# Attention: low parts of three transpose banks per pair on GpSimd instead of VectorE, and GpSimd's other work in another order

## The chip, the cores and the metric

One core of one Trainium2 chip runs the whole program. The metric is the device time of one execution in microseconds (us); the text gives the median of three runs. One further execution was recorded by the hardware profiler, and all rows below come from it.

## The reference

`q`, `k`, `v` are (2, 8, 768, 64): 16 heads. Each head gets a bucket number per token from the signs of six projections, and attention is allowed only inside a bucket. Two feed-forward blocks follow, each on 1536 tokens, 512 wide, with 2048 hidden columns.

```python
q_bits = (einsum('bhsd,dk->bhsk', q, proj) > 0); k_bits = the same of k
mask   = q_bucket[:, :, :, None] == k_bucket[:, :, None, :]
scores = where(mask, D**-0.5 * q @ k.T, -1e9)
attn   = exp(scores - max(scores)); attn = attn / (sum(attn) + 1e-9)
x      = attn @ v                        # to (1536, 512)
h      = maximum(x @ moe_w_in, 0);  x = h * h @ moe_w_out
h      = x @ moe2_w_in;             out = (h / (1 + exp(-h))) @ moe2_w_out
```

Everything is float32. Products take their operands in the fp32r format, so each operand is split into a high part (the value cast to fp32r) and a low part (the value minus its high part), and the products of the parts are added.

## The kernel before

The attention takes the first 250 us of the program, and the change touches only this part. The 16 heads are worked on as 8 pairs. A pair has 4 units (a head and a half of the queries), a unit has 3 score blocks of 128 queries and 6 transposes of 128 keys.

One loop (L897) walks over steps `d` from -5 to 98, and the order in which it emits instructions is the order on every engine; nothing is sorted later. Twelve steps belong to a pair; below, "step 5 of a pair" is `d % 12 == 5`, and the pairs are numbered 0 to 7. A step does, for three stages at once:

- scores of a block (L680, TensorE, into a PSUM tile `s`, of which there are two), the row maximum of the block before (L685, VectorE), two tiny scalar steps (L689, L690), and the exponential (L698, ScalarE) into `P`;
- two **banks**: three 128x128 transposes of `P` each (L713, TensorE, into a PSUM tile `t`, three of them). A bank is copied as high part `th` to SBUF (L718, ScalarE), and VectorE subtracts `th` from the bank in PSUM to get the low part `tl` (L724). Bank `g` of a pair is `g % 24`, so step 5 makes banks 10 and 11, and step 10 makes banks 20 and 21;
- the products with V of the banks made two steps earlier (L737 with `th`, L738 with `tl`, `V_LAG = 4`).

Other work is hung on steps by tables. `todo` is emitted at the end of its step, `mid` (three VectorE operations on weights, L643, L647, L651) just after L690 of a step, `extra` inside it. Step 5 of every pair holds most of the extras: the bucket bits of the next pair (`bits_mm` on TensorE, 12 products, tile `bs`; `bits_cmp` L528 on VectorE), the transposes of the row sums of the pair before (`rb_mm`), the normalisation (`x_norm`, L769), and two `mid` operations on weights in pairs 1 to 6.

GpSimd runs, in the order of emission, what hangs on `todo`: the casts and subtractions that split Q and K of a later pair (`cast_pair` L488, `split_pair` L508), the split of V (`split_v` L617, L618), the loads of K in the layout of the scores (`load_head` L498, a DMA on GpSimd's own queue), the rows of the sums (`norm_rows` L752), `x_sum` L765, `x_put` (L777 to L779 for pairs 0 to 3; five operations, L783 to L787, for pairs 4 and 5), and the preparation of four weight blocks (`w_limit` L639, `wp_put` L660 and L661, `wp_sums` L666 to L669). `w_abs` (L635) of the weight blocks is on ScalarE. SP issues most other DMAs; `place_lo` on SP reads what `split_pair` wrote.

Of the kernel before, what the change touches and what calls it, by code (L numbers as in the profile page):

```python
# [11 lines left out]
F32 = mybir.dt.float32  # L12
F32R = mybir.dt.float32r
# [4 lines left out]
ALU = mybir.AluOpType  # L18
# [8 lines left out]
QW = 384  # L27
# [8 lines left out]
W_LO = float(np.uint32(897 << 20).view(np.float32))  # L36
W_HI = float(np.uint32((1150 << 20) | 0xFFFFF).view(np.float32))
V_LAG = 4
WA = 4
FB = 4  # L40
NP = FB // 2
# [392 lines left out]
def lsh_attention_moe_moe(ctx, tc, kd, qk, v, pc, wi1, wo1, wi2, wo2, out):  # L434
    nc = tc.nc
# [17 lines left out]
    a1 = att.enter_context(tc.tile_pool(name="a1", bufs=1))  # L453
    a2 = att.enter_context(tc.tile_pool(name="a2", bufs=2))
# [252 lines left out]
    PT = {}  # L707
# [6 lines left out]
        PT[g] = (t,)  # L714

    def t_hi(g):
        th = a1.tile([128, QW], F32R, tag="th", bufs=6, name=f"th{g}")
        nc.scalar.copy(out=th, in_=PT[g][0][:, 0:QW])  # L718
        PT[g] += (th,)

    def t_lo(g):
        t, th = PT[g]
        tl = a1.tile([128, QW], F32R, tag="tl", bufs=6, name=f"tl{g}")
        nc.vector.tensor_tensor(out=tl, in0=t[:, 0:QW], in1=th.bitcast(F32), op=ALU.subtract)  # L724
        PT[g] = th, tl
# [19 lines left out]
                nc.sync.dma_start(out=xs[p][i][64 * h : 64 * h + 64, z * QW : (z + 1) * QW], in_=ob[64 * i : 64 * i + 64])  # L745

    def norm_rows(p):
        ri = a2.tile([128, 12], F32, tag="ri", name=f"ri{p}")
        nc.vector.tensor_scalar(out=ri, in0=sums[p], scalar1=1e-9, scalar2=None, op0=ALU.add)
        nc.vector.reciprocal(out=ri, in_=ri)  # L750
        w = rows[p] = a1.tile([128, 6, 2, 64], F32, tag="rw", name=f"rw{p}")
        nc.gpsimd.tensor_copy(out=w, in_=ri.rearrange("p (h c) -> p c h", h=2).unsqueeze(3).broadcast_to([128, 6, 2, 64]))  # L752
# [36 lines left out]
    todo = defaultdict(list)  # L789
# [4 lines left out]
    def at(g, fn, *a):  # L794
        todo[g].append((fn, a))

    for p in range(1, NPAIR):
        d0 = 12 * (p - 1)
        if p > 1:
            at(d0 - 13, load_pair, p)  # L800
            at(d0 - 7, scale_q, p)
            at(d0 - 7, new_hi, p)
            at(d0 - 7, cast_pair, p, 0)
            at(d0 - 6, load_k, p)
            at(d0 - 4, cast_pair, p, 1)
        at(max(d0 - 5, 0), split_pair, p, 0)
        at(max(d0 - 3, 0), split_pair, p, 1)
        extra[d0 + 5].append((bits_mm, bits_cmp, p))
        at(d0 + 1, load_head, p, 0)
        at(d0 + 2, place_lo, p, 0)  # L810
        last[d0 + 5].append((place_bits, (p, 0)))
        at(d0 + 5, load_v, p)
        at(d0 + 11, split_v, p)
        at(d0 + 7, load_head, p, 1)
        at(d0 + 8, place_lo, p, 1)
        at(d0 + 8, place_bits, p, 1)
    for p in range(NPAIR):
        d0 = 12 * (p + 1)
        at(d0 + (2 if p < NPAIR - 1 else -3), norm_rows, p)
        at(d0 + (3 if p < NPAIR - 1 else 2), x_sum, p)  # L820
        if p < NPAIR - 1:
            k = d0 + (5 if p < NPAIR - 2 else 8)
            extra[k].append((rb_mm, x_norm, p))
            at(k + 1, x_put, p)
    for i, (d_load, d_abs, *d_dve) in enumerate(((0, 5, 17, 17, 29), (8, 20, 29, 41, 41), (36, 48, 53, 53, 65), (50, 60, 65, 77, 77))):
        key = (0, 0, i)
        at(d_load, w_load, key)
        at(d_abs, w_abs, key)
        at(d_abs, w_limit, key)
        for d, fn in zip(d_dve, (w_exp, w_sign, w_low)):  # L830
            mid[d].append((fn, key))
        d0 = d_dve[2]
        at(d0 + 1, wp_put, i // 2, i % 2, 2 * (i % 2))
        if i % 2:
            at(d0 + 2, wp_sums, i // 2)
            for h in range(2):
                at(d0 + 3 + h, wp_put, i // 2, h, 4 + 2 * h)
    early = [(0, 1, i) for i in range(WB)]
    for i, key in enumerate(early):
        at(91 + i, w_load, key)  # L840
# [2 lines left out]
    with tc.manual_schedule():  # L843
# [53 lines left out]
        for d in range(-5, G // 2 + 3):  # L897
            ready, new = new, None
            g = 2 * d
            if ready:  # L900
                m = row_max(*ready)
            if 0 <= g - 1 < G:
                t_lo(g - 1)
# [4 lines left out]
            if 0 <= g < G:  # L908
                transp(g)
                t_hi(g)  # L910
                t_lo(g)
                transp(g + 1)
                t_hi(g + 1)
# [4 lines left out]
            for dve, t, p in held[:1]:  # L918
                dve(t, p)
            for n in (g - V_LAG, g + 1 - V_LAG):  # L920
                if 0 <= n < G:
# [15 lines left out]
        p = NPAIR - 1  # L937
# [67 lines left out]
```

## Time and profile before

| | us |
|---|---|
| median of 3 runs | 760.9 (758.87 to 762.92) |
| the profiled execution, its own time | 761.5 |
| its span on the core | 759.7 |
| TensorE busy in the span | 743.8 (98%) |
| VectorE busy | 598.9 (79%) |
| ScalarE busy | 456.4 (60%) |
| GpSimd busy | 409.6 (54%) |

In the rows PE is TensorE's matrix work, PEld its weight loads, DVE VectorE, ACT ScalarE, POOL GpSimd; `out<-in` are the program's tile names. A row of the timeline begins with start and duration in us, and xN at its end counts merged instructions of one kind; the duration is then that of all of them together. A bracket gives the idle time of the engine before the row and what ended it.

### The profile page before, as it was taken

The numbers are of one execution on the slowest core, as the hardware profiler recorded it, in microseconds if no ns is written. First come the engines' busy times: TensorE is split into PE (matmuls) and PEld (weight loads), VectorE is DVE, ScalarE is ACT, GpSimd is POOL, SyncE is SP. The second block draws the span as 40 slices with busy tenths as digits, with TensorE's granted clock in tenths as the row PEclk, the third lists the DMA queues.
The fourth block names the chain that finished last, engine by engine and source line by source line (L and its number), as shares of the span: only waits on it lengthen the run. The fifth ranks groups of instructions, "written<-read, shape, count | busy, mean of one in ns | idle before, by whom it ended". The sixth has DMA issues, their size and how long they took to land.

```text
span 759.7 us, 10882 instructions
## 1 busy us (share of the span) xinstructions
PE 743.8 (98%) x3748; PEld 628.4 (83%) x3748; DVE 598.9 (79%) x1064; ACT 456.4 (60%) x856; POOL 409.6 (54%) x295
## 2 busy tenths in 40 slices
PE   8899999999999989999999999999999999999998
PEld 3689999899999878888888888888788888888887
DVE  4989999999999899658648876999975875685542
ACT  3788988888978776366368349446534625623520
POOL 3454564955763565754564652967566256455200
PEclk8999999999999999999999999999999999999999
DMA  5196765775741412221221221112222031131012
GB/s 151 60 231 151 174 166 155 165 190 147 161 123 43 150 31 80 84 83 57 84 83 56 84 76 41 51 41 80 76 83 84 28 112 37 48 99 40 1 69 98
DMA packets 27382, 71.58 MB, mean 94 GB/s; under 512 B 4208, under 2 KB 8688, under 8 KB 27328
## 3 DMA queue, kind: packets, MB, share of 16 engines
q1 hardware_dynamic: 24984, 64.74, 29.5%
q0 software_dynamic: 2016, 5.51, 3.3%
q10 hardware_dynamic: 328, 0.65, 0.4%
q8 instruction: 30, 0.49, 0.3%
q14 instruction: 24, 0.20, 0.1%
HBM read 49.40 MB, written 3.15 MB: 69 GB/s over the span
## 4 chain that ended last, share of the span: by engine, by line
PE 69%; DVE 20%; POOL 4%; ACT 3%; issue 2%; DMA 2%; SPq 0%; ACTq 0%; DVEq 0%; POOLq 0%
PE bank L336 32%; PE bank L255 17%; PE bank L226 9%; DVE mt L685 5%; DVE tl L724 5%; PE s L680 3%; PE bs L523 2%; PE t L713 2%; DVE ys L149 2%; ACT P L698 2%; PE o L737 2%; PE o L738 1%; DVE xb L155 1%; POOL wp L661 1%; PE warm L858 1%
## 5 line engine op out<-in xcount | busy, mean ns | idle before, releaser
L170 POOL TENSOR_SCALAR wt<-wt 128x512 f32<-128x512 f32 x56 | 117.0, 2099 | 45.2 <-ACT wt L168 45.2
L155 POOL TENSOR_TENSOR wp<-wt,wp 128x512 fp32r<-128x512 f32 x56 | 76.6, 1378 | 96.1 <-ACT wp L153 96.1
L255 PE MATMUL bank<-xb,wp 128*128 128x512 f32 x480 | 111.3, 390 | 2.4 <-DVE ts L260 1.6
L698 ACT ACTIVATE P<-s,mt 128x768 f32<-128x768 f32 x96 | 95.7, 997 | 23.9 <-DVE mt L690 20.5
L255 PEld LDWEIGHTS bank<-xb,wp 128*128 128x128 f32 x480 | 89.7, 188 | 22.6 <-issue 1.5
L724 DVE TENSOR_TENSOR tl<-t,th 128x384 fp32r<-128x384 f32 x192 | 104.9, 548 | 1.9 <-ACT th L718 1.8
L153 ACT CAST wp<-wt 128x512 fp32r<-128x512 f32 x56 | 34.7, 621 | 105.6 <-DVE wt L173 58.1
L685 DVE TENSOR_REDUCE mt<-s 128x1 f32<-128x768 f32 x96 | 91.5, 953 | 8.0 <-PE s L680 7.5
L718 ACT CAST th<-t 128x384 fp32r<-128x384 f32 x192 | 82.3, 485 | 20.3 <-PE t L713 17.8
L680 PE MATMUL s<-kk,qq 76*128 76x384 f32 (+1 forms) x384 | 84.3, 340 | 1.6 <-ACT P L698 0.9
L260 DVE TENSOR_TENSOR ts<-bank,ts 128x512 f32<-128x512 f32 x80 | 54.5, 690 | 36.8 <-PE bank L255 34.1
L713 PE MATMUL t<-ident,P 128*128 128x128 f32 x576 | 81.1, 274 | 1.9 <-DVE tl L724 1.8
L226 PE MATMUL bank<-x0h,wp 128*128 128x512 f32 x256 | 80.2, 389 | 0.0
L713 PEld LDWEIGHTS t<-ident,P 128*128 128x128 f32 x576 | 67.6, 140 | 9.4 <-DVE tl L724 3.3
L737 PE MATMUL o<-th,vv 128*128 128x384 f32 x192 | 72.5, 378 | 2.1 <-POOL vv L618 2.0
L680 PEld LDWEIGHTS s<-kk,qq 76*128 76x128 f32 (+1 forms) x384 | 67.7, 188 | 4.7 <-ACT P L698 2.1
L738 PE MATMUL o<-tl,vv 128*128 128x384 f32 x192 | 64.6, 337 | 0.0
L240 ACT ACTIVATE ts<-bank 128x512 f32<-128x512 f32 x48 | 28.6, 595 | 52.3 <-PE bank L226 26.8
L226 PEld LDWEIGHTS bank<-x0h,wp 128*128 128x128 f32 x256 | 48.1, 188 | 10.0
L155 DVE TENSOR_TENSOR gql<-ts,gqh 128x512 fp32r<-128x512 f32 x64 | 46.2, 734 | 12.7 <-ACT gqh L153 12.4
L172 DVE SCALAR_TENSOR_TENSOR wt<-raw,wt 128x512 uint32<-128x512 uint32 x58 | 51.5, 890 | 0.6
L168 ACT ACTIVATE wt<-raw 128x512 f32<-128x512 f32 x58 | 38.8, 670 | 20.5 <-POOL wp L155 11.0
(153 smaller groups left out, 1713.7 us busy)
## 6 DMA issues: line engine op xcount, KB each, us to landing
raw<-in_dram SPq DMA_DIRECT2D x64, 512.0 KB, 3.3
qq<-hq SPq DMA_DIRECT2D x28, 192.0 KB, 2.7
kk<-in_dram POOLq DMA_DIRECT2D x14, 384.0 KB, 5.2
vr<-in_dram SPq DMA_DIRECT2D x8, 384.0 KB, 3.3
ta<-ob SPq DMA_DIRECT2D x32, 96.0 KB, 3.2
tb<-ob SPq DMA_DIRECT2D x32, 96.0 KB, 3.4
out_dram<-ts SPq DMA_DIRECT2D x11, 256.0 KB, 2.0
rq<-in_dram SPq DMA_DIRECT2D x7, 384.0 KB
```

The costliest lines, as they stand in the source:

```text
L155: add(("DVE", "POOL")[pool], l, lambda: eng.tensor_tensor(out=lo(), in0=src(), in1=hi().bitcast(F32), op=ALU.subtract), (*rk, *hk), lk)
L170: add("DVE" if fast else "POOL", 0.5 if fast else 2.4, lambda: eng.tensor_scalar(out=wtt, in0=wtt, scalar1=W_LO, scalar2=W_HI, op0=ALU.max ...
L226: mm(bank[b], w[:, x, op, sl], t["x0"][y][:, kt], start=kt == 0 and j == 0, stop=kt == 3 and j == 2)
L255: mm(bank[b], w[:, p, op, k * 128 : k * 128 + 128], x[:, q, xop, k], start=first and k == 0 and j == 0, stop=k == 1 and j == 2, skip_group ...
L336: mm(bank[b][:, 0:wd], x, y, start=i == 0 and n == 0, stop=i == FB - 1 and n == 2)
L680: mm(s[:, n, 0:QW], t["qq"][h][0:kk, ab, c0 : c0 + 128], t["kk"][h][0:kk, ab, n * QW : (n + 1) * QW], start=ab == 0, stop=ab == 1)
L685: nc.vector.tensor_reduce(out=m[:, 0:1], in_=s[:, :, 0:QW], op=ALU.max, axis=AX.XY, negate=True)
L698: nc.scalar.activation(out=e.rearrange("p (a b) -> p a b", a=2), in_=s[:, :, 0:QW], func=AF.Exp, scale=m[:, 1:2], bias=m[:, 2:3], accum_ou ...
L713: nc.tensor.transpose(t[:, j * 128 : (j + 1) * 128], P[u, j][:, kt * 128 : (kt + 1) * 128], ident)
L718: nc.scalar.copy(out=th, in_=PT[g][0][:, 0:QW])
L724: nc.vector.tensor_tensor(out=tl, in0=t[:, 0:QW], in1=th.bitcast(F32), op=ALU.subtract)
L737: mm(o[:, 0:QW], vv, th, start=kt == 0, stop=False)
```

## The change

Banks 10, 11 and 20 of each pair are treated in another way. ScalarE copies the whole bank as plain float32 into a new SBUF tile `tf` (two buffers); GpSimd casts `tf` to `th` and subtracts to `tl`. VectorE's L724 is not emitted for these banks.

The tables move: the second `cast_pair` from step 8 to step 10 of a pair and the second `split_pair` from step 9 to step 11; `split_v` from step 11 to step 8. `w_abs` with `w_limit` of blocks 1, 2 and 3 go from `d` = 20, 48, 60 to 21, 51, 57, and stand first in their step's `todo`. The `wp_put` and `wp_sums` move from one step after the last VectorE operation of their block to the step of it and to 4, 7 and 8 steps after it (before: 1, 2, 3 and 4). The tile `ri` has one buffer instead of two.

```diff
+BY_POOL = (10, 11, 20)
...
     def t_hi(g):
+        if g % 24 in BY_POOL:
+            tf = a1.tile([128, QW], F32, tag="tf", bufs=2, name=f"tf{g}")
+            nc.scalar.copy(out=tf, in_=PT[g][0][:, 0:QW])
+            th = a1.tile([128, QW], F32R, tag="th", bufs=6, name=f"th{g}")
+            tl = a1.tile([128, QW], F32R, tag="tl", bufs=6, name=f"tl{g}")
+            nc.gpsimd.tensor_copy(out=th, in_=tf)
+            nc.gpsimd.tensor_tensor(out=tl, in0=tf, in1=th.bitcast(F32), op=ALU.subtract)
+            PT[g] = th, tl
+            return
...
     def t_lo(g):
+        if g % 24 in BY_POOL:
+            return
...
-        ri = a2.tile([128, 12], F32, tag="ri", name=f"ri{p}")
+        ri = a1.tile([128, 12], F32, tag="ri", name=f"ri{p}")
...
-            at(d0 - 4, cast_pair, p, 1)
+            at(d0 - 2, cast_pair, p, 1)
...
-        at(max(d0 - 3, 0), split_pair, p, 1)
+        at(max(d0 - 1, 0), split_pair, p, 1)
...
-        at(d0 + 11, split_v, p)
+        at(d0 + 8, split_v, p)
...
-    for i, (d_load, d_abs, *d_dve) in enumerate(((0, 5, 17, 17, 29), (8, 20, 29, 41, 41), (36, 48, 53, 53, 65), (50, 60, 65, 77, 77))):
+
+    for i, (d_load, d_abs, *d_dve) in enumerate(((0, 5, 17, 17, 29), (8, 21, 29, 41, 41), (36, 51, 53, 53, 65), (50, 57, 65, 77, 77))):
...
-        at(d_abs, w_abs, key)
-        at(d_abs, w_limit, key)
+        todo[d_abs][0:0] = [(w_abs, (key,)), (w_limit, (key,))]
...
-        at(d0 + 1, wp_put, i // 2, i % 2, 2 * (i % 2))
+        at(d0, wp_put, i // 2, i % 2, 2 * (i % 2))
         if i % 2:
-            at(d0 + 2, wp_sums, i // 2)
+            at(d0 + 4, wp_sums, i // 2)
             for h in range(2):
-                at(d0 + 3 + h, wp_put, i // 2, h, 4 + 2 * h)
+                at(d0 + 7 + h, wp_put, i // 2, h, 4 + 2 * h)
```

## Rows read from the trace of the kernel before

**Rows 1.** Busy us of each engine in a stretch: PE, PEld, DVE, ACT, POOL.

```profile
60.00:90.00 30.00, 29.81 (x201) 27.93 (x199) 29.57 (x71) 26.23 (x59) 15.99 (x14) 1.00 0.68 164
```

**Rows 2.** Timeline of PE: steps 5 of two pairs, then the two long steps.

```profile
95.32 0.38 PE L523 MATMUL bs<-hq,pjh 128*48 128x384 f32 x1 [0.19 <-ACT P L698]
...
99.58 0.82 PE L713 MATMUL t<-ident,P 128*128 128x128 f32 x6
...
101.63 0.82 PE L713 MATMUL t<-ident,P 128*128 128x128 f32 x6
...
123.39 0.38 PE L523 MATMUL bs<-hq,pjh 128*48 128x384 f32 x1 [0.19 <-ACT P L698]
...
127.82 0.82 PE L713 MATMUL t<-ident,P 128*128 128x128 f32 x6
...
140.98 0.34 PE L738 MATMUL o<-tl,vv 128*128 128x384 f32 x1
...
144.25 0.94 PE L713 MATMUL t<-ident,P 128*128 128x128 f32 x6
...
146.89 0.45 PE L737 MATMUL o<-th,vv 128*128 128x384 f32 x1 [1.71 <-POOL vv L618]
...
148.40 0.82 PE L713 MATMUL t<-ident,P 128*128 128x128 f32 x6
...
230.70 0.82 PE L713 MATMUL t<-ident,P 128*128 128x128 f32 x6
...
233.38 0.82 PE L713 MATMUL t<-ident,P 128*128 128x128 f32 x6
```

**Rows 3.** Timeline of DVE: two row maxima, then step 5 of pair 3.

```profile
62.27 0.90 DVE L685 TENSOR_REDUCE mt<-s 128x1 f32<-128x768 f32 x1
...
64.18 0.95 DVE L685 TENSOR_REDUCE mt<-s 128x1 f32<-128x768 f32 x1
...
124.10 0.68 DVE L647 SCALAR_TENSOR_TENSOR wi<-raw,wi 128x512 uint32<-128x512 uint32 x1
...
125.90 1.06 DVE L528 TENSOR_SCALAR bt<-bs,pcr 48x768 fp32r<-48x768 f32 x1
```

**Rows 4.** POOL's groups from 60 to 230 us: busy us, mean ns | idle before.

```profile
L661 POOL TENSOR_TENSOR wp<-wi,wp 128x512 fp32r<-128x512 f32 x8 | 10.3, 1290 | 0.6
...
L660 POOL CAST wp<-wi 128x512 fp32r<-128x512 f32 x8 | 4.9, 609 | 0.1
...
L779 POOL COPY ys<-ta 128x256 f32<-128x256 f32 x4 | 1.6, 395 | 0.0
...
L666 POOL TENSOR_TENSOR wi<-wi 128x256 f32<-128x256 f32 x2 | 1.5, 740 | 0.0
```

**Rows 5.** Timeline of ACT: copies of banks 10 and 11 of pair 3; `w_abs`.

```profile
123.23 0.86 ACT L718 CAST th<-t 128x384 fp32r<-128x384 f32 x2
...
142.97 0.66 ACT L635 ACTIVATE wi<-raw 128x512 f32<-128x512 f32 x1
```

**Rows 6.** Timeline of POOL in pair 3 and the start of pair 4.

```profile
127.89 0.62 POOL L777 CAST x0h<-ta 128x512 fp32r<-128x512 f32 x1 [0.96 <-DVE ta L769]
...
130.17 0.61 POOL L660 CAST wp<-wi 128x512 fp32r<-128x512 f32 x1
...
132.10 0.63 POOL L498 DMA_DIRECT2D kk<-in_dram  x1
...
134.56 0.73 POOL L666 TENSOR_TENSOR wi<-wi 128x256 f32<-128x256 f32 x1
...
144.12 0.83 POOL L617 CAST vv<-vr 128x768 fp32r<-128x768 f32 x1
...
146.81 1.92 POOL L639 TENSOR_SCALAR wi<-wi 128x512 f32<-128x512 f32 x1
```

**Rows 7.** Timeline of POOL and DVE where both work from SBUF.

```profile
300.16 3.24 POOL L155 TENSOR_TENSOR wp<-wt,wp 128x512 fp32r<-128x512 f32 x2 [1.48 <-ACT wp L153]
...
301.07 1.18 DVE L172 SCALAR_TENSOR_TENSOR wt<-raw,wt 128x512 uint32<-128x512 uint32 x1
```

## The prediction

> **What bounds the kernel now.** I read the summary of engines first, then busy time by stretches, then the timeline of each engine over one pair, and last the idle time that TensorE shows in front of single rows. The summary says that TensorE is busy nearly throughout; the stretch says that in the attention VectorE is so too, 29.57 us of 30 beside TensorE's 29.81, while GpSimd works for 15.99 [rows 1]. So the question is which of the two sets the pace, because the change takes time from VectorE alone. A plain step takes 101.63 - 99.58 = 2.05 us on TensorE, with its fourteen products and transposes one behind the other [rows 2]. VectorE can do a step in less: behind the two small operations of `norm_rows` it was late, and its next two row maxima began 64.18 - 62.27 = 1.91 us apart [rows 3]. Its spare time is 0.14 us in each step, filled by waits too short to see. TensorE is the bound of plain steps, and VectorE's relief there buys nothing.
>
> What is to be had is TensorE's idle time. In step 2 of pair 4 the first product with the new V waits for `split_v`, which GpSimd reaches late: the step takes 148.40 - 144.25 = 4.15 us, 2.10 too long. In pair 7 the same place costs 233.38 - 230.70 - 2.05 = 0.63 [rows 2]. Both pairs follow one with `wp_sums`. And step 5, from `bs` to the next transposes, takes 99.58 - 95.32 = 4.26 us in most pairs, but 127.82 - 123.39 = 4.43 in pair 3 (and as much in pair 6), where two long weight operations and bank 10's subtraction push `bits_cmp` back to 125.90 [rows 2, 3].
>
> **The change part by part.** All is worked against the profiled execution (761.5 us, 0.6 above the median of 760.9). T is the start of `bs` in step 5 of a pair, 123.39 in pair 3.
>
> *Removed.* (a) `split_v` three steps earlier: V is split by T + 14 and needed some 8 us later, so both waits go: -2.10 - 0.63. (b) 24 subtractions leave VectorE. In step 10 and at the start of step 6 they stand in plain steps: 0. In step 5 `bits_cmp` must wait for `bs` anyway; only pairs 3 and 6 lose their extra 0.17: -0.34.
>
> *Added on ScalarE.* The copy to `tf` takes the place of the copy to `th`, same size, 0.43 us: 0.
>
> *Added on GpSimd.* No row has 384 columns. Casts take 0.395 us (256) and 0.609 (512), subtractions 0.740 and 1.290 [rows 4], so I take 0.50 and 1.02, 1.53 us per bank with the gaps; the bounds are 1.14 and 1.90. A bank's `th` and `tl` are due two steps later. Banks 10 and 11 start when the copy is there, T + 0.36 [rows 5], end at T + 3.4, and are due after T + 6: in time. Bank 20 is queued behind all that steps 5 to 9 hang on GpSimd. In pair 3, in the new order: cast of the next Q 0.8, `wp_put` 1.93 (132.10 - 130.17), `x_put` 2.28 (130.17 - 127.89), load of K and a split 2.46 (134.56 - 132.10), `split_v` 2.69 (146.81 - 144.12) [rows 6], `wp_sums` four times 0.74 with gaps 3.1 [rows 4], and the bank: T + 18.2. TensorE takes bank 20's `tl` at 140.98, T + 17.6 [rows 2], 17.4 without the 0.17. With 0.1 for the signal it is late by 0.9. Pair 5 has no sums but the long `x_put`, three subtractions and two casts, 5.1 [rows 4]: T + 17.9, late by 0.55. Pair 6 has both, without the next Q and K: T + 18.4, late by 1.05. Pairs 1, 2 and 4 come to T + 15.1, in time by 2.3. So +2.5; with the bounds of a bank, three banks in each chain, +0.4 to +5.8.
>
> *Added contention.* In the rows of before the two weight operations of step 5 run while GpSimd is idle; now GpSimd reads banks 10 and 11 from SBUF at just that time. Where both worked from SBUF, a weight operation that takes 0.68 us alone [rows 3] took 1.18, until GpSimd's first subtraction had ended [rows 7]. In step 5 the first weight operation comes at T + 0.71, GpSimd's subtraction of bank 10 at T + 0.94: it waits for the first operation until about T + 1.3, and the second operation waits for it until T + 2.3. Then `bits_cmp`, due at T + 2.3, starts at T + 2.6 in pairs 1, 2, 4, 5 and T + 2.9 in pairs 3 and 6, and the next scores wait for the PSUM tile that it frees: 4 x 0.25 + 2 x 0.5 = 2.0. GpSimd loses 0.7 to 0.95 to the same operations, TensorE 0.25 to 0.5, so bank 20 is later by another 0.45 in three pairs: 1.4. If the second weight operation slips in ahead of GpSimd, TensorE loses nothing in step 5, but bank 20 comes about 1 us later, with the same sum. I take +3.0 of the 3.4; the bounds are 0 (no overlap hurts) and 5.8 (the price of a whole subtraction, 0.97 more, in six pairs).
>
> The Trainium skill, "SBUF — State Buffer", section "Who interferes with whom", says more than these rows: VectorE with two SBUF inputs contends with any GpSimd instruction that reads SBUF, a cast as well, and the loser waits for the whole instruction. By that the casts of banks 10 and 11 would also shut out a weight operation, and the sum would have some 0.3 us more in each of six pairs; no row above shows a cast against such an operation.
>
> *Moved.* `w_abs` of block 2 goes from step 0 to the end of step 3 of pair 4: 0.66 us on ScalarE [rows 5], ahead of the copies of banks 8 and 9 and of the exponential for which `bs` waits (95.32, [rows 2]). `bs` follows ScalarE there directly, so it should cost nearly all of it, +0.5 (bounds 0 and 0.66). Blocks 1 and 3 move between places of one kind: 0. The second `cast_pair` and `split_pair` end two steps later; behind them on SP is `place_lo` in step 2 of the next pair, which then starts about a microsecond after `split_pair`; its data are needed from step 7. The load of K on GpSimd's queue in step 1 and the rows of sums in step 2 come behind the moved `wp_put` in pairs 4 and 7, earlier than in the trace of before, where they stood behind the late split. In pair 4 a `wp_put` may now meet the small `norm_rows` operations on VectorE: +0.3 (0 to 1.1). At the end of pair 7, with short steps, bank 20 is tight: +0.1.
>
> Sum: -2.10 - 0.63 - 0.34 + 2.5 + 3.0 + 0.5 + 0.3 + 0.1 = +3.3. On the median: 760.9 + 3.3 = 764.2. Half a per cent, 3.8 us, is about what a measurement of this kernel tells from no change: the forecast is a loss just inside it.
>
> **The rivals.**
>
> *GpSimd keeps up (758 to 762).* For it: GpSimd is idle for almost half of its time [rows 1], and the late bank 20 is a difference of some 18 us of summed rows; 5% less and it vanishes. Then the sum is -3.1 + 0.5 and what is left of contention: 761.5 - 2.6 = 758.9 without any, 761.9 with 3.0, on the median 758.3 to 761.3. Against it: the chains have no gaps in rows 6.
>
> *VectorE was the bound (747 to 756).* If steps follow VectorE, 24 subtractions at some 0.47 us from start to start give 11 us beside the 2.7: 747. For it: VectorE's 29.57 of 30. Against it: the 1.91 us of rows 3. At half of the price, 753.
>
> *GpSimd becomes the bound in every pair: slower (767 to 776).* Place: bank 20 of all six pairs with weight work. It decides when banks and contention take over 2.3 us more than the costed T + 15.1 of the lighter pairs. At that point the three late pairs lose 1.6 each above what is summed, 761.5 + 3.3 + 4.8 = 769.6; a microsecond more costs all six one each: 775. For it: the row of rows 7, in which GpSimd's two subtractions take 3.24 instead of 2.6, is a stretch of 25%. Against it: every GpSimd row of the attention is near its group's mean.
>
> **How the numbers follow.** My own case (762 to 767) 0.52, GpSimd keeps up 0.26, VectorE the bound 0.08, GpSimd the bound 0.14. Own case: 0.28 within half a per cent (up to 764.7), 0.24 above. So faster 0.08; same 0.28 + 0.26 = 0.54; slower 0.24 + 0.14 = 0.38. The range 757.5 to 768.5 holds the first two cases and the lower edge of the last, about 0.82.
>
> **What would show it.** Right: no wait of TensorE for V; a wait of L738 for GpSimd's `tl` in step 0 behind pairs 3, 5 and 6 of about 1 us each; weight operations of step 5 longer than 0.69 us; the step from `bs` to the transposes above 4.26 in pairs 1 to 6; plain steps still 2.05. Wrong: plain steps under 2.05 (VectorE was the bound), waits for `tl` of banks 10 and 11, or bank 20 never waited for.

## The result and the profile after

| | us |
|---|---|
| after, median of 10 runs | 765.26 (763.85 to 766.67) |
| before, in the same comparison, median of 10 runs | 761.22 (758.87 to 763.58) |
| ratio | 1.0052, 95% interval 1.0039 to 1.0064 |
| profiled execution of after, its own time and its span | 763.85; 762.0 |

The change costs 4.0 us, half a per cent. The forecast was 764.2 in a range of 757.5 to 768.5, a loss just inside half a per cent; it came out just outside.

GpSimd is busy for 38 us more (409.6 to 447.7), VectorE for only 4 less (598.9 to 595.0). The summary of the changed kernel:

```profile
PE 744.6 (98%) x3748; PEld 629.8 (83%) x3748; DVE 595.0 (78%) x1040; ACT 458.1 (60%) x856; POOL 447.7 (59%) x343
```

VectorE's groups in the attention (busy us, mean ns of one | idle before) show where a part of the relief went. The weight operations of step 5, 0.69 us or less each before, are longer, L644 (0.42 alone) above all:

```profile
L736 DVE TENSOR_TENSOR tl<-t,th 128x384 fp32r<-128x384 f32 x168 | 91.6, 547 | 2.4 <-ACT th L728 2.2
...
L644 DVE TENSOR_SCALAR wi<-wi 128x512 uint32<-128x512 uint32 x4 | 4.7, 1172 | 0.0
L652 DVE SCALAR_TENSOR_TENSOR wi<-raw,wi 128x512 uint32<-128x512 uint32 x4 | 4.2, 1060 | 0.1
...
L648 DVE SCALAR_TENSOR_TENSOR wi<-raw,wi 128x512 uint32<-128x512 uint32 x4 | 3.7, 928 | 0.1
```

The waits of TensorE in the attention of after (first column total us, then times, then the longest) have lost the wait for V and gained one for `tl` of GpSimd:

```profile
PEld o L750 <- POOL tl L724: 2.9, 4, 0.9
...
PE o L750 <- POOL tl L724: 1.9, 3, 0.6
...
PE o L749 <- POOL th L723: 0.3, 1, 0.3
```

The first line counts weight loads and the other two products of the same places, so they don't add up; the fourth load is that of bank 20 at the end of pair 7. To see the whole price I measured the length of each step on TensorE, from its first product with V to that of the next step. From step 2 to step 95 that is 217.63 us before and 222.55 after; the 4.92 us fall on these steps:

| steps | after minus before, us |
|---|---|
| the two that waited for V (pairs 4 and 7) | -2.61 |
| behind the bucket products, pairs 1, 2, 3, 5, 6 and the end of pair 7 | +1.12 |
| pair 4: the bucket step and the one behind it | +0.96 |
| bank 20 of pairs 3, 5, 6, two steps each | +3.77 |
| `norm_rows` in pairs 4 and 7, which the wait for V had covered | +0.39 |
| around `w_abs` of blocks 1 and 3 (9 steps) | +0.27 |
| 45 plain steps | +0.70 |
| first six steps | +0.27 |
| the rest | +0.04 |

The two feed-forward blocks are alike, so the step lengths and the start of the loop carry the difference. The start differs for a reason of its own. These are busy time and granted clock of the first 30 us (the eighth figure is PEclk), before and then after:

```profile
0.00:30.00 30.00, 24.51 (x92) 12.05 (x92) 17.39 (x38) 13.84 (x23) 9.45 (x15) 0.89 0.34 96
```

```profile
0.00:30.00 30.00, 24.28 (x104) 13.00 (x105) 21.24 (x46) 15.76 (x28) 12.10 (x16) 1.00 0.35 96
```

In before's recorded execution TensorE ran at the lower of its two levels, 1.2 GHz, for some 6.8 us of its warm-up; in after's it did not. The loop began at 31.61 us there and at 28.97 here. So the two recorded executions differ by only 2.35 us (763.85 - 761.5), the loop by 4.92, and the medians, with starts of all kinds in them, by 4.04. Below I compare loops and medians, not spans.

The loop of one execution is not exact either. The kernel before, recorded a second time, has a loop of 219.65, 2.02 more: behind its wait for V the granted clock was at the lower level for 3.4 us, and step 7 took 0.46 more. In step 7 TensorE can wait for a DMA (`kk<-bt`: 0.57 us in before, 1.03 in its repeat, none in the kernel with the tile places alone), and the step takes 2.33 to 3.90 in the kernels below; so the +0.27 of the first six steps can't be laid to the change. Executions with the same mean granted clock differ by about as much as the loops do: at 0.998, nine executions of before beside the experiments average 759.59, and three of after 764.59.

**Step 5.** Pair 3 of after answers to [rows 2, 3, 5]; T, the start of `bs`, is 121.88. Timelines of POOL, of DVE and of PE (start, duration, ..., idle before and its cause):

```profile
122.26 0.51 POOL L723 CAST th<-tf 128x384 fp32r<-128x384 f32 x1 [1.90 <-ACT tf L720]
122.85 1.34 POOL L724 TENSOR_TENSOR tl<-tf,th 128x384 fp32r<-128x384 f32 x1
124.14 0.96 POOL L723 CAST th<-tf 128x384 fp32r<-128x384 f32 x1
125.18 1.00 POOL L724 TENSOR_TENSOR tl<-tf,th 128x384 fp32r<-128x384 f32 x1
126.13 0.83 POOL L489 CAST hq<-rq 128x768 fp32r<-128x768 f32 x1
```

```profile
122.58 0.73 DVE L648 SCALAR_TENSOR_TENSOR wi<-raw,wi 128x512 uint32<-128x512 uint32 x1
123.35 1.39 DVE L652 SCALAR_TENSOR_TENSOR wi<-raw,wi 128x512 uint32<-128x512 uint32 x1
124.66 1.06 DVE L529 TENSOR_SCALAR bt<-bs,pcr 48x768 fp32r<-48x768 f32 x1
```

```profile
121.88 0.38 PE L524 MATMUL bs<-hq,pjh 128*48 128x384 f32 x1 [0.20 <-ACT P L699]
...
125.78 0.97 PE L681 MATMUL s<-kk,qq 128*128 128x384 f32 x4 [0.25 <-DVE bt L529]
126.59 0.82 PE L714 MATMUL t<-ident,P 128*128 128x128 f32 x6
```

GpSimd's subtraction of bank 10 is 0.34 us longer than that of bank 11, which nothing disturbs: it waits for the end of L648 (123.31). Then L652 waits for that subtraction (124.19), and the cast of bank 11 waits for L652 (124.74). They take turns, and each one's time is the next one's wait. `bits_cmp` starts at T + 2.78, against 125.90 - 123.39 = 2.51 in [rows 2, 3], and the transposes come 4.71 us after `bs` instead of 4.43.

**Bank 20.** The rest of GpSimd's chain in the same pair, then TensorE, which answers to the row at 140.98 of [rows 2]:

```profile
138.68 0.73 POOL L670 TENSOR_TENSOR wi<-wi 128x256 f32<-128x256 f32 x1
139.36 0.50 POOL L723 CAST th<-tf 128x384 fp32r<-128x384 f32 x1
139.94 1.00 POOL L724 TENSOR_TENSOR tl<-tf,th 128x384 fp32r<-128x384 f32 x1
```

```profile
139.02 0.82 PE L714 MATMUL t<-ident,P 128*128 128x128 f32 x6
139.91 0.44 PE L749 MATMUL o<-th,vv 128*128 128x384 f32 x1
140.99 0.44 PE L750 MATMUL o<-tl,vv 128*128 128x384 f32 x1 [0.64 <-POOL tl L724]
...
142.31 0.82 PE L714 MATMUL t<-ident,P 128*128 128x128 f32 x6
```

The step takes 142.31 - 139.02 = 3.29 us, 1.22 more than its plain neighbours. A part comes from `th`, which is late too (139.91, where the steps beside it have 0.57 after the transposes); the row shows only the last wait.

### The profile page after: what moved, and what is told of

The parts are those of the page before. It is cut to its first block, busy times and chain, and to the rows that moved or that the text cites. A ratio compares the mean times of both kernels' runs of the same rounds, so it can differ in the third digit from the quotient of the medians.

```text
span 762.0 us, 10895 instructions
## 1 busy us (share of the span) xinstructions
PE 744.6 (98%) x3748; PEld 629.8 (83%) x3748; DVE 595.0 (78%) x1040; ACT 458.1 (60%) x856; POOL 447.7 (59%) x343
## 4 chain that ended last, share of the span: by engine, by line
PE 57%; DVE 6%; issue 0%; DVEq 0%
PE bank L337 32%; PE bank L256 16%; PE bank L227 9%; DVE ys L150 1%; DVE xb L156 1%; DVE wt L173 1%; DVE wt L172 1%; DVE wt L174 1%; DVE ts L261 1%; DVE x0l L156 0%; DVE g0l L156 0%; DVE y L351 0%; DVE ys L351 0%; DVE wt L211 0%; DVE gql L156 0%
## 5 line engine op out<-in xcount | busy, mean ns | idle before, releaser
L736 DVE TENSOR_TENSOR tl<-t,th 128x384 fp32r<-128x384 f32 x168 | 91.6, 547 | 2.4 <-ACT th L728 2.2
L728 ACT CAST th<-t 128x384 fp32r<-128x384 f32 x168 | 72.5, 485 | 23.0 <-PE t L714 20.6
```

## The experiments

All ratios are against the kernel before, run beside each kernel on the same chip. Step lengths are TensorE's, as above.

**The new order alone** leaves all banks on VectorE.

```diff
-BY_POOL = (10, 11, 20)
+BY_POOL = ()
```

> The changed kernel with no bank on GpSimd (the list of banks is empty): the new order of GpSimd's work alone. My theory: the order gains and the banks lose. TensorE's waits for V in pairs 4 and 7 go (-2.1 and -0.6), no wait for bank 20, step 5 back at 4.26 and 4.43 us except in pair 4, where the moved w_abs costs 0.76 as in the changed kernel; plain steps 2.05 if the 2.07 of the changed kernel comes with its banks or their tiles. Sum -2.0: 759.2, ratio to before 0.997. Rival (the new order is what loses, VectorE's relief is worth something): at or above the kernel before, 761 to 764.

Measured: 761.17, ratio 0.9997 (0.9983 to 1.0011). The waits for V are gone (-2.61), and yet the time is that of before; I had expected 2 us of gain. Pair 4 costs 1.25, `norm_rows` in pairs 4 and 7 0.36, plain steps 0.70. Of the 1.25 in pair 4, 0.51 lie in the bucket step: `w_abs` stands ahead of the exponential on ScalarE, and the bucket products wait for that exponential longer. The products in before and in this kernel:

```profile
153.52 0.37 PE L523 MATMUL bs<-hq,pjh 128*48 128x384 f32 x1 [0.20 <-ACT P L698]
```

```profile
150.96 0.37 PE L524 MATMUL bs<-hq,pjh 128*48 128x384 f32 x1 [0.60 <-ACT P L699]
```

The other 0.74, in the step behind, are not `w_abs` itself. Here is step 5 of the pair, POOL and DVE:

```profile
148.90 1.92 POOL L640 TENSOR_SCALAR wi<-wi 128x512 f32<-128x512 f32 x1 [2.33 <-ACT wi L636]
...
150.80 1.83 POOL L777 TENSOR_TENSOR ta<-ta,tb 128x768 f32<-128x768 f32 x1
151.18 1.74 DVE L644 TENSOR_SCALAR wi<-wi 128x512 uint32<-128x512 uint32 x1
...
154.03 1.06 DVE L529 TENSOR_SCALAR bt<-bs,pcr 48x768 fp32r<-48x768 f32 x1
```

`w_limit` (L640), hung behind the moved `w_abs`, holds up `x_sum` (L777), and that now lies in step 5, where VectorE's L644, 0.42 us alone, waits for its end and takes 1.74.

**The banks alone**, with the old order (every table entry taken back; two of them are shown):

```diff
-        at(d0 + 8, split_v, p)
+        at(d0 + 11, split_v, p)
...
-            at(d0 + 4, wp_sums, i // 2)
+            at(d0 + 2, wp_sums, i // 2)
```

> The kernel before, in its old order, with banks 10, 11 and 20 on GpSimd: the banks alone. My theory: without the new order GpSimd's queue is fuller ahead of bank 20 (wp_sums and a wp_put come before it, and so does the second split), so TensorE waits for bank 20 about 5 us in pair 3, 3 us in pair 6 and 1 us in pair 5, while the waits for V there shrink or go; step 5 is 0.2 to 0.3 longer in six pairs. 769, between 766 and 771. Rival (the order is what loses, the banks gain by VectorE's relief): below the kernel before, 757 to 760.

Measured: 772.47, ratio 1.0146 (1.0130 to 1.0163), above what I had expected. Behind pair 3 bank 20 stands at the end of a queue that now holds four sums and three `wp_put` ahead of it. Rows of PE in this kernel:

```profile
141.85 0.82 PE L714 MATMUL t<-ident,P 128*128 128x128 f32 x6
146.45 0.69 PE L749 MATMUL o<-th,vv 128*128 128x384 f32 x1 [3.78 <-POOL th L723]
147.52 0.69 PE L750 MATMUL o<-tl,vv 128*128 128x384 f32 x1 [0.39 <-POOL tl L724]
149.93 1.48 PE L714 MATMUL t<-ident,P 128*128 128x128 f32 x6
153.38 0.82 PE L714 MATMUL t<-ident,P 128*128 128x128 f32 x6
```

The products after the wait are slow, because the granted clock had fallen to 0.50, and the next two steps took 4.61 and 2.89 us. Behind pair 6 the wait is shorter (the step that ends with it takes 4.41, behind pair 3 it takes 6.10), the clock stayed full, and the next two steps took 2.98 and 2.07. The difference of 2.45 us is most of the 3.5 that the expectation lacked. With the new order the banks cost 7.2 us less than without it (772.47 - 765.26).

**The tile places alone.** The kernel before, with `tf` reserved but unused and `ri` in one buffer:

```diff
+        if g in (10, 11):
+            a1.tile([128, QW], F32, tag="tf", bufs=2, name=f"tf{g}")
...
-        ri = a2.tile([128, 12], F32, tag="ri", name=f"ri{p}")
+        ri = a1.tile([128, 12], F32, tag="ri", name=f"ri{p}")
```

> The kernel before with the two tf tiles allocated at the same place and never used, and ri in one buffer, so that V, hq, ob, bt and the sums lie at the addresses of the changed kernel; nothing else differs. The plain step of TensorE was 2.054 us before and 2.072 in the changed kernel, which no term of the prediction has. If addresses in SBUF make it, this kernel has 2.07 too and is 1.4 us slower than before (762.6). Rival (GpSimd's or ScalarE's work on the banks makes it, or the run): 2.054 and the time of before, 761.2.

Measured: 761.61, ratio 1.0005 (0.9992 to 1.0017). Plain steps are 2.07 us, as in after, with no instruction of the change in the kernel. The loop comes out at 217.65, as before, though most of its steps are longer, 0.80 us in all: the slower steps shorten the waits for V by 0.23 (4.00 and 2.52 instead of 4.12 and 2.64), and step 7 took 0.55 less in this execution. On the medians a loss of that size lies inside the interval. So the lengthening comes from where tiles lie or from the single `ri`, not from GpSimd's work on banks; in after, where the wait for V is gone, it is paid in full. The kernel with the new order alone has no `tf` at all and takes 2.07 as well, so `tf` is not needed for it.

**`w_abs` of block 2 two steps earlier:**

```diff
-    for i, (d_load, d_abs, *d_dve) in enumerate(((0, 5, 17, 17, 29), (8, 21, 29, 41, 41), (36, 51, 53, 53, 65), (50, 57, 65, 77, 77))):
+    for i, (d_load, d_abs, *d_dve) in enumerate(((0, 5, 17, 17, 29), (8, 21, 29, 41, 41), (36, 49, 53, 53, 65), (50, 57, 65, 77, 77))):
```

> The changed kernel with w_abs and w_limit of weight block 2 in step 49 instead of 51 (step 1 of pair 4, as early as its buffer allows). My theory: the 0.76 us that pair 4's step 5 has above the other pairs (6.22 against 5.46) come from w_abs standing in front of the exponential for which the bucket products wait; they go, and step 2 or so of pair 4 has 0.1 to 0.3 more: 764.7 against 765.3. Rival (pair 4's step 5 is long for another reason, GpSimd's w_limit or the weights): step 5 stays at 6.2 and the time at 765.3.

Measured: 765.76, ratio 1.0052 (1.0036 to 1.0068). The pair's two steps are back at 5.19 and 2.13 (after: 5.72 and 2.57), which shows that `w_abs` with `w_limit` is the cause; but step 50 now takes 2.59 instead of 2.07. The ScalarE operation costs 0.5 in either place, and the loop gains 0.5 only (222.02). On the medians such a difference can't be seen.

**The kernel before again**, for its plain steps:

> The kernel before, unchanged, profiled once more. Every variant so far has plain steps of 2.07 us, also the one with only the tiles moved, and the first profile of the kernel before has 2.054. If the place of the tiles in SBUF makes the difference (the single ri tile shifts V, ob and hq in all variants), this run has 2.054 again. If it belongs to the chip or the run, this run has 2.07, and 1.2 us of the difference between the two first profiles are no effect of the change.

Measured: 761.91 in one run, plain steps 2.054 us as before. So 2.07 is no matter of one execution. (Its longer loop, 219.65, comes from other steps, as said above.) PE of this run and then of after, from one step's score products to the next transposes:

```profile
101.89 0.86 PE L680 MATMUL s<-kk,qq 128*128 128x384 f32 x4
102.59 0.82 PE L713 MATMUL t<-ident,P 128*128 128x128 f32 x6
...
104.64 0.82 PE L713 MATMUL t<-ident,P 128*128 128x128 f32 x6
```

```profile
101.33 0.88 PE L681 MATMUL s<-kk,qq 128*128 128x384 f32 x4
102.04 0.82 PE L714 MATMUL t<-ident,P 128*128 128x128 f32 x6
...
104.12 0.82 PE L714 MATMUL t<-ident,P 128*128 128x128 f32 x6
```

104.64 - 102.59 = 2.05 against 104.12 - 102.04 = 2.08; the score products are the ones that take longer.

**One part of the banks at a time.** Banks 12 and 13, which fall into step 6, in place of all three; bank 20 alone; banks 10 and 11 alone:

```diff
-BY_POOL = (10, 11, 20)
+BY_POOL = (12, 13)
```

> The changed kernel with banks 12 and 13 (step 6) on GpSimd instead of 10, 11 and 20. As many banks as in step 5 leave VectorE, but the weight operations of step 5 meet no bank. Theory (contention in SBUF): the step behind the bucket products is as in the kernel with the new order alone (2.14 in pairs 1, 2, 5 and 2.30 in pairs 3 and 6), against 2.31 to 2.33 and 2.58 in the changed kernel; no wait for a bank; 761.2, as the new order alone. Rival (GpSimd's share of work as such slows VectorE or TensorE, wherever it stands): 2.3 and 2.58 stay, 762.3.

```diff
-BY_POOL = (10, 11, 20)
+BY_POOL = (20,)
```

> The changed kernel with bank 20 alone on GpSimd. Theory: bank 20 is late in pairs 3, 5 and 6 only because banks 10 and 11 and the contention stand ahead of it in GpSimd's queue (3.9 us); without them it comes at T + 14.3 where T + 17.4 is due, and TensorE waits nowhere for it: 761.2, as the new order alone. Rival (a bank's two hops over ScalarE and GpSimd in two steps are too long as such): the waits of about 1 us stay, 764.

```diff
-BY_POOL = (10, 11, 20)
+BY_POOL = (10, 11)
```

> The changed kernel with banks 10 and 11 alone on GpSimd. Theory: the contention of step 5 stays (2.31, 2.33, 2.58, 2.57, 2.33, 2.58 us behind the bucket products), the waits for bank 20 go: 1.0 us above the new order alone, 762.2. Rival (the loss of step 5 comes from all three banks together, or from GpSimd being late): 761.2.

Measured: 762.82 (1.0012, 0.9996 to 1.0029), 761.59 (1.0008, 0.9987 to 1.0029) and 763.23 (1.0011, 0.9996 to 1.0027). None of the three can be told from before, but their steps tell the parts apart. The step behind the bucket products, pairs 1 to 6:

| | us |
|---|---|
| before | 2.14 2.14 2.31 2.14 2.14 2.30 |
| after | 2.31 2.33 2.58 2.57 2.33 2.58 |
| 10 and 11 alone | 2.31 2.31 2.59 2.58 2.33 2.57 |
| 20 alone | 2.14 2.14 2.30 2.90 2.14 2.31 |
| 12 and 13 | 2.14 2.14 2.30 2.87 2.14 2.31 |

So this loss is made by banks 10 and 11 and by nothing else (pair 4 has the `x_sum` as well). And in these kernels TensorE waits for bank 20 behind pairs 3, 5 and 6 only when all three banks are there: with bank 20 alone it just comes in time. POOL and PE of that kernel in pair 3:

```profile
127.81 0.82 POOL L489 CAST hq<-rq 128x768 fp32r<-128x768 f32 x1 [4.81 <-ACT rq L493]
...
141.01 0.50 POOL L723 CAST th<-tf 128x384 fp32r<-128x384 f32 x1
141.59 1.01 POOL L724 TENSOR_TENSOR tl<-tf,th 128x384 fp32r<-128x384 f32 x1
```

```profile
142.50 0.42 PE L749 MATMUL o<-th,vv 128*128 128x384 f32 x1
142.75 0.34 PE L750 MATMUL o<-tl,vv 128*128 128x384 f32 x1
```

`tl` is done at 142.60, 0.15 us before it is taken. The expectation had it 3.1 us early, because it counted banks 10 and 11 with their contention as 3.9 us of GpSimd's queue. But without them the cast of the next Q, which heads the queue, still waits for ScalarE's scaling of that Q. It starts at T + 2.70 here (T is 125.11) and at T + 4.25 in after, so the two banks delay the queue by 1.55 us only.

Without bank 20 a new collision appears in step 51: 3.33 us with banks 10 and 11 alone. With banks 12 and 13 the steps 51 and 87 take 2.67 and 3.05, which the expectation did not have. POOL and DVE in step 51 with banks 10 and 11 alone:

```profile
147.78 1.28 POOL L662 TENSOR_TENSOR wp<-wi,wp 128x512 fp32r<-128x512 f32 x1
147.83 1.26 DVE L761 TENSOR_SCALAR ri<-sums 128x12 f32<-128x12 f32 x1
```

A VectorE operation on 12 columns takes 1.26 us: it sits out GpSimd's subtraction, which ends at 149.06. This is the meeting of `wp_put` and `norm_rows` that the prediction priced at 0 to 1.1; in after itself the small operation is done at 146.76, just before that subtraction starts at 146.81.

**The sums later:** `wp_sums` behind bank 20.

```diff
-            at(d0 + 4, wp_sums, i // 2)
+            at(d0 + 6, wp_sums, i // 2)
```

> The changed kernel with wp_sums two steps later (step 11 of pairs 3 and 6, behind bank 20, instead of step 9). Theory: the waits for bank 20 in pairs 3 and 6 are GpSimd's queue and nothing else; 3.1 us leave the queue ahead of it, so the 1.2 and 1.5 us go, and pair 5's 0.96 stays: 2.7 less, 762.6. Rival (the waits come from the contention of step 5 or from ScalarE's copy): they stay, 765.3.

Measured: 763.83, ratio 1.0030 (1.0014 to 1.0046). The waits for bank 20 behind pairs 3 and 6 are gone (2.07); pair 5, which has no sums, keeps its 2.99. The loop is 220.39, 2.16 less than after, although step 7 took 0.42 more; the four steps around the two waits are 2.71 shorter, as expected. Two of the three late places hang on the 3 us of sums ahead of them, as the prediction's chain had it.

**Putting the pieces together.** First the new order without the banks, `ri` with two buffers again, and `w_abs` with `w_limit` of blocks 1, 2 and 3 earlier; then `norm_rows` with one operation less (1e-9 is not added to the sums); then also the load of weight block 3 at step 43 instead of 50. Each difference is against the kernel named before it, the first against after:

```diff
-BY_POOL = (10, 11, 20)
+BY_POOL = ()
...
-        ri = a1.tile([128, 12], F32, tag="ri", name=f"ri{p}")
+        ri = a2.tile([128, 12], F32, tag="ri", name=f"ri{p}")
...
-    for i, (d_load, d_abs, *d_dve) in enumerate(((0, 5, 17, 17, 29), (8, 21, 29, 41, 41), (36, 51, 53, 53, 65), (50, 57, 65, 77, 77))):
+    for i, (d_load, d_abs, *d_dve) in enumerate(((0, 5, 17, 17, 29), (8, 17, 29, 41, 41), (36, 49, 53, 53, 65), (50, 53, 65, 77, 77))):
```

> The new order without banks on GpSimd, ri again in two buffers (all tiles lie as in the kernel before), and w_abs with w_limit of blocks 1, 2 and 3 in steps 17, 49 and 53 instead of 21, 51 and 57: blocks 1 and 3 in step 5 of a pair, where ScalarE waits 2 us for transposes. Theory: plain steps back at 2.054 if the place of the tiles makes them longer (-1.2 against the order alone); pair 4 without the 0.5 before its bucket products and the 0.75 behind them, where x_sum, pushed into step 5 by w_limit, held the weight operation; 0.3 each less in pairs 1 and 4; 0.5 more in step 50. Sum against the order alone -2.6: 758.6, below both kernels. Rival on the steps: 2.07 stays, 759.8.

```diff
-        nc.vector.tensor_scalar(out=ri, in0=sums[p], scalar1=1e-9, scalar2=None, op0=ALU.add)
-        nc.vector.reciprocal(out=ri, in_=ri)
+        nc.vector.reciprocal(out=ri, in_=sums[p])
```

> As e10_order, and norm_rows takes the reciprocal of the sums at once: the addition of 1e-9 is left out (the sums are at least 1, so it changes no bit of them in float32). VectorE has one small operation less in step 2 of each pair, 0.17 to 0.2 us. The step there takes 2.23 to 2.25 us because the two operations, 0.35, exceed VectorE's spare time of 0.14. Theory: one operation of 0.23 leaves at most 0.09: seven steps of 2.05 to 2.14, 0.8 to 1.2 less than e10_order, 757.6. Rival (the 0.2 are not VectorE's lateness): no difference to e10_order.

```diff
-    for i, (d_load, d_abs, *d_dve) in enumerate(((0, 5, 17, 17, 29), (8, 17, 29, 41, 41), (36, 49, 53, 53, 65), (50, 53, 65, 77, 77))):
+    for i, (d_load, d_abs, *d_dve) in enumerate(((0, 5, 17, 17, 29), (8, 17, 29, 41, 41), (36, 49, 53, 53, 65), (43, 53, 65, 77, 77))):
```

> As e11_order_ri (1e-9 not added), with weight block 3 loaded in step 43 instead of 50. In e10 and e11 ScalarE waits 3.5 us in step 53 of the loop for that load before w_abs, and two steps of TensorE are 0.2 to 0.4 and 0.8 us longer. Theory: the load has landed and both go, 1.0 to 1.2 us: 757.4. Rival (the two steps are long by VectorE's weight operations behind x_sum): 758.5 as e11.

Measured: 759.39 (0.9974, 0.9960 to 0.9987), 758.49 (0.9960, 0.9947 to 0.9973) and 757.33 (0.9941, 0.9921 to 0.9961). Beside runs of the kernel before at 761.71, 761.71 and 762.48, all three beat both kernels. In the first, plain steps are 2.054 again. It differs from the new order alone in the buffers of `ri` and in the steps of `w_abs`, and neither kernel has `tf`. The kernel with the tile places alone has 2.07 with `w_abs` in its old steps, so the longer plain steps go with the single buffer of `ri`. Step 50, where `w_abs` of block 2 now stands, takes 2.26, 0.2 more and not the 0.5 of the kernel further above. In the second the `norm_rows` steps fall from 2.25 to 2.05. The second also shows the price of taking a thing earlier; ACT in pair 4:

```profile
156.98 0.66 ACT L636 ACTIVATE wi<-raw 128x512 f32<-128x512 f32 x1 [3.50 <-DMA raw<-in_dram]
```

`w_abs` of block 3, moved to step 53, waits 3.50 us for its weights, and with it all of ScalarE; TensorE's steps 53 and 54 take 2.53 and 2.89 us. With the load seven steps earlier the wait is gone and step 54 takes 2.05. Step 53 stays at 2.54, against the expectation: L644 takes 0.92 there, because `x_sum` on GpSimd runs until 151.31, 0.63 into it, which is the rival that was named for both steps. Of the gain of 0.59% in the last kernel, 0.26 are the new order without banks, with two buffers of `ri` and the earlier `w_abs`; the rest is `norm_rows` and the load.

## Why the prediction was right

*The bound.* Right. With 24 subtractions off VectorE no plain step got shorter, and TensorE stays 98% busy. Only step 6 of pair 0, where TensorE had waited 0.49 us for VectorE's `tl`, fell from 2.76 to 2.43, and the wait for the DMA in step 7 took that back. VectorE as the bound (747 to 756) is excluded by the steps, and so is GpSimd as the bound of every pair: pairs 1, 2 and 4 never wait for bank 20.

*V split earlier, -2.73.* Right: -2.61; of the rest, 0.04 are the two longer plain steps, and the steps here are measured from another product.

*A bank on GpSimd, 0.50 and 1.02 us, 1.53 with gaps.* Right: 0.50 and 1.00 where nothing disturbs, 140.88 - 139.36 = 1.52 from cast to next work.

*Bank 20 late in pairs 3, 5 and 6, +2.5, and another 1.4 through contention.* Right in place, number and size: +3.77 against 3.9, and by pair 1.27, 0.99 and 1.51 against 1.35, 1.00 and 1.50. In pair 3 the chain ends at T + 19.06, forecast T + 18.2 + 0.45. The step that started it, the cast of the next Q, begins at T + 4.25 where the forecast had T + 3.4: GpSimd loses 0.85 us in step 5 (0.34 of it on one subtraction and 0.46 on a cast), as bounded there (0.7 to 0.95). Bank 20 alone and the later sums confirm the chain by taking away either end of it. One bound was summed wrongly: three banks at 0.39 less each take 1.17 off a chain, more than any of the three was late, so the lower bound was 0 and not +0.4. The 0.1 for bank 20 at the end of pair 7 came out at 0.16, in step 96 (0.85 instead of 0.69), behind the stretch of the table.

*Contention in step 5, +2.0, less 0.34 for `bits_cmp`.* Right in mechanism, somewhat too large: 0.17 to 0.28 a pair, +1.1 in five pairs. The order of events was as written: first weight operation at T + 0.70 (forecast 0.71), subtraction at T + 0.97 (0.94), second operation held until T + 2.31 (2.3). Only `bits_cmp` came at T + 2.78 instead of T + 2.9. The gain of 0.34 from the lost subtraction can't be told apart from it; banks 10 and 11 alone show the net.

Beside this the prediction weighed the Trainium skill, "SBUF — State Buffer", section "Who interferes with whom", by which casts too contend. The trace agrees with that: the cast of bank 11 waits for L652 and takes 0.96 instead of 0.50 us. It also agrees with what the section says of the order of issue: here the cast came second, so it was the one to wait, and the extra 0.3 us in each pair did not come. The cast of bank 10 came first, and ran 0.19 us into L648, which took 0.73 instead of 0.68.

*`w_abs` of block 2, +0.5.* Right for what it counted: the bucket step of pair 4 takes 5.72 instead of 5.19. But pair 4 lost 0.96, and 0.43 of that lies in the step behind, where 0.25 was summed as contention. What failed is that the term counted ScalarE alone. `w_limit` follows `w_abs` on GpSimd and pushes `x_sum` into step 5; the new order alone loses 0.74 there without any bank, and with both at step 49 that step is back at 2.13, even with banks 10 and 11 on GpSimd.

*`norm_rows` against `wp_put`, +0.3.* +0.39, but by another way: in pairs 4 and 7 the wait for V had covered what `norm_rows` costs in every pair (2.25 instead of 2.05). The collision that was meant showed up only in the kernels with banks 10 and 11 alone and with banks 12 and 13. That the number came out near is luck.

*"Plain steps still 2.05."* Wrong: 2.07, which costs 0.70 in the 45 plain steps. This was in no case of the prediction. It comes with the single buffer of `ri`, a part of the change that the prediction gave no cost: with it (and an unused `tf`) the instructions of before take 2.07, without `tf` it is 2.07 too, and with two buffers it is 2.054. No instruction of a plain step uses `ri`, so the likely way is that the tiles behind it lie elsewhere. Which tile that is, and why the score products feel it, stays open; no run moved single tiles.

The forecast's sum is +3.3; measured are +4.9 in the loop and +4.0 on the medians. Of the 1.6 us in the loop, 0.70 are the plain steps, not foreseen; 0.27 are the first six steps, which vary by more than that between two executions of before; 0.27 lie around `w_abs` of blocks 1 and 3, costed at nothing; what pair 4 and bank 20 took above their terms is nearly what contention took below its own. On the medians the sum was 0.7 us short, with single terms of 2 to 4 us of both signs in it.

## What to carry to other kernels

Work that is moved to an idle engine is not free while its operands lie where another engine works: ask which operations will run at the same moment, and count the turns that they take. A queue in order has to be summed from a fixed moment to the due time of its last item, with all that hangs on it; that sum gave the three late places out of six here, and moving 3 us of other work behind the item cured two. And when a stall goes, look at what it had covered: `norm_rows` and a part of the longer plain steps had cost nothing in the two pairs where V was late.

## What the runs showed of the hardware that was not expected

- A small operation waits as long as a large one: 12 columns on VectorE, 0.17 us alone, took 1.26 us beside a GpSimd subtraction of 1.28, and 0.59 when they met it half way (banks 12 and 13).
- TensorE's clock can fall after a wait in mid-program. In the kernel with the banks alone TensorE was busy for 1.17 us of the four from 144 to 148, and the granted clock was 0.50 (1.2 GHz) until 152; in the repeat of before, the wait for V was followed by a mean of 0.72 from 146 to 152 and a step of 3.27 us; in before's first recorded execution the same wait was followed by none. Stretches of the kernel with the banks alone, then one of the repeat of before (busy us of PE, PEld, DVE, ACT, POOL, then PEclk):

```profile
144.00:148.00 4.00, 1.17 (x2) 0.77 (x3) 0.12 (x1) 1.32 (x3) 3.84 (x6) 0.76 0.01 3
148.00:152.00 4.00, 4.00 (x16) 3.90 (x16) 1.83 (x5) 0.96 (x2) 3.92 (x4) 0.50 0.01 2
```

```profile
146.00:152.00 6.00, 6.00 (x31) 5.88 (x31) 2.96 (x8) 2.83 (x8) 4.86 (x4) 0.72 0.94 217
```

- One buffer less of a tile that the step does not touch (`ri`) went with a step of fourteen products and transposes of 2.07 us instead of 2.054; the four score products took the difference.
